# Moving the stage tiles and the weights' pool to multiples of 512 bytes in SBUF

## The chip, the cores and the metric

The kernel runs on one core of a Trainium2 chip. The metric is the device time of one execution in microseconds, the median of three runs. The engines of the core are TensorE (PE, with its weight loads listed apart as PEld), VectorE (DVE), ScalarE (ACT), GpSimd (POOL) and SyncE (SP), which here only issues DMAs. SBUF is the on-chip memory: 128 partitions, and in each of them a tile occupies a run of bytes that begins at some offset. All partitions of a tile use the same offset, so "address" in this document means the offset within a partition.

## The reference

Sparse attention with a local window and some global positions, followed by a feed-forward layer. For batch 8, 8 heads, 512 local and 32 global positions and head size 64:

```
s_g  = scale * q_g @ [k_g, k_l].T ;  out_g = softmax(s_g) @ [v_g, v_l]
s_l  = [scale * q_l @ k_g.T, scale * q_l @ k_l.T where |i - j| <= 32 else -1e9]
out_l = softmax(s_l) @ [v_g, v_l]
x = concat([out_g, out_l]) as 4608 tokens x 512
h = x @ w_in                      # 512 -> 2048
g = max(h, 0) + alpha * min(h, 0)
out = g @ w_out                   # 2048 -> 512
```

Everything is float32 in and out. The weights come to the kernel as 64-bit floats, and the kernel decodes them.

## The kernel before, in words

The feed-forward layer is the bulk of the work. Its tokens are handled in nine groups: one for each batch entry (512 columns) and one for all global positions (256 columns). Each group has 16 steps over the hidden size. In a step `f1` (line 395) computes 128 hidden features: twelve matmuls of 128 x 128 weights and 512 (or 256) moving columns into the PSUM tile `h_ps`. To keep float32 accuracy with a faster number format (`float32r`), each operand is split into a high and a low part: `xh` and `xl` for the activations, `wt[:, 0]` and `wt[:, 1]` for the weights; three products of the four are summed. DVE then applies the activation function (lines 407 and 408, tile `g`), ACT rounds it to `gh` (line 410), and POOL computes the remainder `gl` (line 411). Two steps later `f2` (line 414) multiplies `gh` and `gl` with the second weight matrix, twelve matmuls again, into four PSUM tiles `o0` to `o3` which accumulate over the 16 steps. At the end of a group they are copied to `ost` and written out.

The attention for the next groups runs between these steps. Its queries and keys arrive in `rawq` and `rawk` (line 156), are split into `hi` and `kl` (lines 186 to 199), and give scores of 192 or 224 columns (line 219). Probabilities lie in `p_sb` and, transposed, in `pt_sb`; the values lie in `vt`. For the first eight pairs of heads unsplit operands are used, from the tile `qk_raw` that shares the buffers of `hi`. The tile `gn` holds what the global queries need.

The weights are decoded while the first steps run: a DMA brings 64-bit words to `wraw` (line 105), ACT, DVE and POOL turn them into a float32 stage tile (lines 113 to 120), and `split_weights` (line 123) writes the high and the low part to `wt`. Both `wraw` and `wt` come from the weights' pool, 33 buffers of 4096 bytes per partition, which later also lends buffers to `rawk`.

The order of the instructions on each engine comes from a planner that simulates the program; parts of it are pinned to the written order (from step 36 on, line 561), and the attention's parts get a higher priority (line 551). All DMAs are issued from SP's queue.

Where a tile lies follows from the order of the pools and of the tiles in them, each size rounded up to 32 bytes. At the bottom are 256 bytes for DMA descriptors and four constants of 32 bytes each, so the first tile of the kernel, `alpha_sb`, lies at 384. Its 64 bytes are followed by `mask` (896), `p_sb` (7168), `pt_sb` (10240), `sg_sb` (1152), `x_raw` (8192) and `x_glb` (4096). Then come the 18 stage tiles of 2048 bytes (line 99: one tag `st` for `xh`, `xl`, `g`, `gh`, `gl`, `ost`, `vx`, and the weights under decoding), two buffers of 4864 for `hi`, nine small tiles of 32, `gn` (2432), `vt` (4096), six small tiles of 32 and three of 128, `rawq` (2048), two buffers of 2560 for `kl`, and last the pool of the weights. Added up, that gives:

| tile | address before | past a multiple of 512 |
|---|---|---|
| `p_sb`, `pt_sb`, `sg_sb` | 1344, 8512, 18752 | 320 |
| `x_raw`, `x_glb` | 19904, 28096 | 448 |
| stage tiles | 32192 + 2048 n | 448 |
| `hi`, two buffers | 69056, 73920 | 448, 192 |
| `gn` | 79072 | 224 |
| `vt` | 81504 | 96 |
| `rawq`, `kl` | 86176, 88224, 90784 | 160 |
| weights' pool | 93344 + 4096 n | 160 |

In `hi` the queries come first and the keys start 2048 bytes later; block i of the queries starts 512 i bytes in, and the four blocks of keys start 0, 128, 288 and 448 columns of 4 bytes in.

Of the kernel before, what the change touches and what calls it, by code (L numbers as in the profile page):

```python
# [8 lines left out]
F32 = mybir.dt.float32  # L9
# [10 lines left out]
NF = DF // 128  # L20
# [25 lines left out]
GS = (2, "mid")  # L46
EV = dict(pt0=(2, "mid"), pt1=(4, "pre"), ptg=(4, "pre"), pv0=(5, "mid"), pv1=(6, "mid"))
SM = (2, "post")
RATE = ((1, 1, 0), (2, 1))
GROUPS = [("l", b) for b in range(NB)] + [("g", 0)]  # L50

# [9 lines left out]
def longformer_ffn(ctx: ExitStack, tc: tile.TileContext, qk, qkr, gn, vt, vx, w, alpha, out):  # L61
# [3 lines left out]
    const = ctx.enter_context(tc.tile_pool(name="const", bufs=1))  # L65
    work = ctx.enter_context(tc.tile_pool(name="work", bufs=1))
# [1 line left out]

    dram = ctx.enter_context(tc.tile_pool(name="dram", bufs=1, space=bass.MemoryType.DRAM))
    wpool = ctx.enter_context(tc.tile_pool(name="wpool", bufs=NWB))  # L70
    alpha_sb = const.tile([128, NF], F32, name="alpha_sb")
    mask = const.tile([128, 224], F32, name="mask")
    p_sb = const.tile([128, 1792], F32, name="p_sb")
    pt_sb = const.tile([128, 2, 4, 2, 160], F32, name="pt_sb")
# [79 lines left out]
    raws, vts, vxs, gns = {}, {}, {}, {}  # L154
# [11 lines left out]
        raws[P, h, part] = raw  # L166

    def load_gn(P):
        gns[P] = work.tile([128, 608], F32, tag="gn", name="gn", bufs=1)
        b, p = divmod(P, NPAIR)  # L170
        nc.sync.dma_start(gns[P], gn[b, p])

# [97 lines left out]
    def global_softmax(P):  # L270
        s = gbank.pop(P)
        m, z = small("gm"), small("gz")
        nc.vector.tensor_reduce(m[:, 0:1], s[:, 0:288], axis=AX.X, op=ALU.max)
        nc.vector.tensor_scalar(m[:, 1:2], m[:, 0:1], -0.125, None, op0=ALU.mult)
        nc.vector.tensor_copy(m[0:64, 0:1], m[64:128, 1:2])
        nc.vector.tensor_tensor(m[0:64, 1:2], m[0:64, 1:2], m[0:64, 0:1], op=ALU.min)
        nc.vector.tensor_copy(m[64:128, 1:2], m[0:64, 1:2])
        nc.scalar.activation(sg_sb, s[:, 0:288], AF.Exp, bias=m[:, 1:2], scale=0.125, accum_out=z[:, 0:1])
        nc.vector.tensor_copy(z[0:64, 1:2], z[64:128, 0:1])
        nc.vector.scalar_tensor_tensor(z[0:64, 1:2], z[0:64, 1:2], 1e-9, z[0:64, 0:1], op0=ALU.add, op1=ALU.add)  # L280
        nc.vector.reciprocal(z[0:64, 1:2], z[0:64, 1:2])
        nc.vector.tensor_copy(z[64:128, 1:2], z[0:64, 1:2])
        nc.scalar.activation(sg_sb, sg_sb, AF.Copy, scale=z[:, 1:2])  # L283
# [90 lines left out]
    def pv_out(P, first, last):  # L374
        b, p = divmod(P, NPAIR)
        nc.scalar.copy(x_raw[:, p, 0:384].rearrange("d (i q) -> d i q", i=3), first[:, 0:480].rearrange("p (i q) -> p i q", i=3)[:, :, 0:128])
        nc.scalar.copy(x_raw[:, p, 384:512], last[:, 0:128])
        xg = x_glb[:, p, SG * b : SG * b + SG]
        nc.vector.tensor_reduce(xg, sub_ap(first, 0, 128, 128, ((1, 32), (160, 3))), axis=AX.X, op=ALU.add)
        nc.vector.tensor_tensor(xg, xg, last[:, 128:160], op=ALU.add)  # L380
# [60 lines left out]
    def live(P):  # L441
        return 0 <= P < NPR
# [3 lines left out]
    def glob(P, s, where):  # L446
        if GS == (s, where):
# [3 lines left out]
            elif P >= NRAW and (live(P) or live(P - 1)):  # L451
# [6 lines left out]
                if P > NRAW:  # L458
                    pv_out(P - 1, first, last)
        if live(P) and SM == (s, where):  # L460
            global_softmax(P)
# [34 lines left out]
    def attn_mid(u):  # L496
        P, s = divmod(u, 4)
        glob(P, s, "mid")
        while tails:
            tails.pop()()  # L500
        raw_events(u, "mid")
        if s == 0 and live(P):
            load_gn(P)
        if s == 0 and live(P + 1):
            if P + 1 < NRAW:
                load_pair(P + 1)
            else:
                load_qk(P + 1, 0, 0)
                load_qk(P + 1, 0, 1)
        if s == 1 and P == NRAW:  # L510
            for c0 in (0, 864):
                nc.gpsimd.memset(sub_ap(p_sb, 0, 128, c0, ((896, 2), (1, 32))), 0.0)
        if s == 2:
            if P == NRAW:
                nc.gpsimd.memset(sub_ap(pt_sb, 0, 128, 1280 + 512, ((640, 2), (1, 128))), 0.0)
            if live(P):
                load_v(P)
# [18 lines left out]
    def weights_step(u):  # L536
        k = state[0]
        n = RATE[0][u % len(RATE[0])] if u < NPRE else RATE[1][u % len(RATE[1])]
        new = [i for i in range(k, min(k + n, len(pieces)))]
# [120 lines left out]
```

## Time and profile before

| | us |
|---|---|
| median of three runs | 1040.6 (1039.6 to 1041.49) |
| span of the profiled execution, first to last instruction | 1038.9 |
| PE busy | 992.1 (96%) |
| DVE busy | 681.0 (66%) |
| ACT busy | 497.4 (48%) |
| POOL busy | 410.6 (40%) |
| mean granted PE clock | 0.977 |

The page's span is that of one profiled execution; the median lies 1.7 us above it. A busy time counts an instruction from its start to its end, and matmuls overlap, so how fast PE works is read from the distance between starts, not from the duration of one matmul. In a timeline row the first number is the start, the second the time from the first start to the last end of the merged instructions, and the count stands at the end. In a row of a group, the numbers after the bar are the busy time in us, the mean duration of one instruction in ns, and the idle time of the engine before them with what ended it.

### The profile page before, as it was taken

Reading aid. Unit: us, or ns where it says so; the run is one execution under the profiler, and the core shown is the slowest. Engines: PE = TensorE matmul, PEld = TensorE weight load, DVE = VectorE, ACT = ScalarE, POOL = GpSimd, SP = SyncE. Lnnn points to the kernel's source line nnn. Section 1 sums busy time; section 2 is a strip of 40 time slices with the busy share of each in tenths; the row PEclk is TensorE's granted clock in tenths of the full one; section 3 lists DMA queues with packets and bytes.
Section 4 is the critical chain, followed back from the end, with each engine's and each line's share of the span. In section 5 each row is a group of like instructions: output and inputs, shape, how many; then the busy total and the mean of one; then the engine's idle time right before and its main releaser. Section 6 shows DMA issues by size and latency. Waiting matters only on the chain.

```text
span 1038.9 us, 17103 instructions
## 1 busy us (share of the span) xinstructions
PE 992.1 (96%) x5592; PEld 791.2 (76%) x5592; DVE 681.0 (66%) x2162; ACT 497.4 (48%) x1331; POOL 410.6 (40%) x330
## 2 busy tenths in 40 slices
PE   6798989898999999999999999999999999999998
PEld 3455767676888878887888788878887788888798
DVE  8987788866666766676667666776667666322322
ACT  5466466665455554455455554555455543201121
POOL 6620466663344343333444433334443431122222
PEclk9896898998999999999999999999999999999999
DMA  9454232135444554455455555445445543100010
GB/s 335 175 187 172 103 126 86 56 94 161 148 148 141 160 149 148 140 161 157 148 149 151 165 150 148 141 149 151 148 144 159 146 126 92 41 1 1 1 42 21
DMA packets 95274, 133.00 MB, mean 128 GB/s; under 512 B 10192, under 2 KB 53712, under 8 KB 95184
## 3 DMA queue, kind: packets, MB, share of 16 engines
q1 hardware_dynamic: 95184, 131.91, 40.7%
q8 instruction: 44, 0.72, 0.3%
q14 instruction: 46, 0.38, 0.1%
HBM read 100.93 MB, written 30.93 MB: 127 GB/s over the span
## 4 chain that ended last, share of the span: by engine, by line
PE 77%; DVE 14%; DMA 3%; ACT 2%; issue 2%; POOL 1%; SPq 0%; ACTq 0%; DVEq 0%; POOLq 0%
PE o L93 33%; PE h_ps L93 31%; PE o_ps L93 6%; PE s_ps L93 4%; PE g_ps L93 3%; DVE wt L118 2%; DVE wt L115 2%; DVE rz L211 1%; DVE wt L117 1%; DMA rawq<-in_qk_dram 1%; DVE p_sb L246 1%; DVE g L408 1%; DMA out_dram<-ost 1%; DVE g L407 1%; DVE pt_sb L321 1%
## 5 line engine op out<-in xcount | busy, mean ns | idle before, releaser
L93 PE MATMUL h_ps<-xh,wt 128*128 128x512 f32 (+1 forms) x1152 | 352.2, 389 | 4.3 <-DVE g L408 3.9
L411 POOL TENSOR_TENSOR gl<-g,gh 128x512 fp32r<-128x512 f32 (+1 forms) x144 | 178.2, 1237 | 436.8 <-ACT gh L410 405.1
L93 PE MATMUL o<-gh,wt 128*128 128x512 f32 (+1 forms) x1152 | 282.4, 386 | 1.6 <-ACT ost L305 1.6
L93 PEld LDWEIGHTS o<-gh,wt 128*128 128x128 f32 x1152 | 204.5, 188 | 50.3 <-ACT ost L305 6.6
L93 PEld LDWEIGHTS h_ps<-xh,wt 128*128 128x128 f32 x1152 | 207.3, 191 | 44.6 <-DVE g L408 4.1
L93 PE MATMUL h_ps<-xl,wt 128*128 128x512 f32 (+1 forms) x576 | 222.6, 388 | 0.9 <-DVE xl L390 0.9
L410 ACT CAST gh<-g 128x512 fp32r<-128x512 f32 (+1 forms) x144 | 85.9, 596 | 266.4 <-DVE g L408 243.2
L407 DVE TENSOR_SCALAR g<-h_ps,alpha_sb 128x512 f32<-128x512 f32 (+1 forms) x144 | 103.2, 717 | 121.2 <-PE h_ps L93 120.4
L217 ACT ACTIVATE p_sb<-p_sb,rz 128x192 f32<-128x192 f32 (+1 forms) x252 | 101.3, 451 | 131.8 <-DVE rz L212 129.7
L93 PE MATMUL o<-gl,wt 128*128 128x512 f32 (+1 forms) x576 | 150.6, 382 | 0.0
L250 ACT ACTIVATE p_sb<-p_sb,mn 128x224 f32<-128x224 f32 (+2 forms) x256 | 115.0, 451 | 40.3 <-DVE mn L246 39.8
L93 PEld LDWEIGHTS h_ps<-xl,wt 128*128 128x128 f32 x576 | 109.3, 190 | 25.6 <-issue 1.3
L93 PEld LDWEIGHTS o<-gl,wt 128*128 128x128 f32 x576 | 104.5, 187 | 23.8 <-issue 0.5
L211 DVE TENSOR_SCALAR rz<-z 128x2 f32<-128x2 f32 x128 | 52.5, 411 | 91.3 <-ACT p_sb L250 90.2
L300 DVE STREAM_TRANSPOSE pt_sb<-sg_sb 32x64 f32<-32x64 f32 x384 | 90.7, 236 | 27.4 <-ACT sg_sb L283 21.2
L408 DVE SCALAR_TENSOR_TENSOR g<-h_ps,g 128x512 f32<-128x512 f32 (+1 forms) x144 | 93.9, 652 | 2.9
L196 POOL TENSOR_TENSOR hi<-rawq,hi 64x512 fp32r<-64x512 f32 x48 | 62.2, 1295 | 83.4 <-DMA vt<-in_vt_dram 50.0
L93 PE MATMUL o_ps<-pt_sb,vt 128*64 128x160 f32 (+4 forms) x832 | 72.3, 298 | 11.9 <-DVE mn L246 8.0
L199 POOL TENSOR_TENSOR kl<-rawk,hi 128x640 fp32r<-128x640 f32 x48 | 76.2, 1587 | 3.7
L93 PEld LDWEIGHTS o_ps<-pt_sb,vt 128*64 128x64 f32 (+2 forms) x832 | 50.3, 140 | 32.5 <-issue 12.2
L246 DVE CUSTOM_DVE_ANT_0 p_sb<-s_ps,mask 128x192 f32<-128x192 f32 x192 | 64.1, 362 | 11.1 <-PE s_ps L93 9.9
L120 POOL TENSOR_TENSOR wt<-wt,wr 128x512 int32<-128x512 int32 x32 | 43.2, 1352 | 66.2 <-DVE rz L211 38.1
(86 smaller groups left out, 1042.3 us busy)
## 6 DMA issues: line engine op xcount, KB each, us to landing
scratch<-p_sb SPq DMA_DIRECT2D x192, 112.0 KB, 2.3
wraw<-in_w_dram SPq DMA_DIRECT2D x32, 512.0 KB, 6.9
vt<-in_vt_dram SPq DMA_DIRECT2D x32, 512.0 KB, 5.0
rawk<-in_qk_dram SPq DMA_DIRECT2D x96, 160.0 KB, 2.9
rawq<-in_qk_dram SPq DMA_DIRECT2D x96, 128.0 KB, 2.7
pt_sb<-scratch SPq DMA_DIRECT2D x48, 256.0 KB, 2.8
gn<-in_gn_dram SPq DMA_DIRECT2D x32, 304.0 KB, 5.4
pt_sb<-scratch SPq DMA_DIRECT2D x48, 192.0 KB, 2.9
```

Source lines behind the costliest of these rows:

```text
L93: ins = nc.tensor.matmul(*a, **k)
L196: nc.gpsimd.tensor_tensor(q, raw[64:128], q.bitcast(F32), op=ALU.subtract)
L199: nc.gpsimd.tensor_tensor(kl[P, h], raw, t.bitcast(F32), op=ALU.subtract)
L211: nc.vector.tensor_scalar(rz[:parts, 0:n], z[:parts, 0:n], 1e-9, None, op0=ALU.add)
L217: nc.scalar.activation(r, r, AF.Copy, scale=rz[:parts, e : e + 1])
L246: nc.vector.tensor_tensor_reduce(out=pr, in0=s[:, 256 * e : 256 * e + nn], in1=masks[e], scale=-0.125, scalar=3.0e38, op0=ALU.add, op1=ALU ...
L250: nc.scalar.activation(pr, pr, AF.Exp, bias=mn[:, e : e + 1], scale=-1.0, accum_out=z[:, e : e + 1])
L300: nc.vector.transpose(dst, src)
L407: nc.vector.tensor_scalar(g[:, 0:n], h[:, 0:n], 0.0, alpha_sb[:, f : f + 1], op0=ALU.min, op1=ALU.mult)
L408: nc.vector.scalar_tensor_tensor(g[:, 0:n], h[:, 0:n], 0.0, g[:, 0:n], op0=ALU.max, op1=ALU.add)
L410: nc.scalar.copy(gh[:, 0:n], g[:, 0:n])
L411: nc.gpsimd.tensor_tensor(gl[:, 0:n], g[:, 0:n], gh[:, 0:n].bitcast(F32), op=ALU.subtract)
```

## The change

Two tiles are made larger, and only their first part is used, so that everything allocated behind them moves up: `alpha_sb` by 64 bytes and `gn` by 288. What is read and written, by which instruction, in which order and with which waits stays the same.

```
+PAD = (16, 72)
...
-    alpha_sb = const.tile([128, NF], F32, name="alpha_sb")
+    alpha_sb = const.tile([128, NF + PAD[0]], F32, name="alpha_sb")[:, 0:NF]
...
     def load_gn(P):
-        gns[P] = work.tile([128, 608], F32, tag="gn", name="gn", bufs=1)
+        gns[P] = work.tile([128, 608 + PAD[1]], F32, tag="gn", name="gn", bufs=1)[:, 0:608]
```

All tiles from `mask` to `gn` move by 64 bytes, those behind `gn` by 352. The stage tiles then begin at 32256, which is 63 x 512, and the weights' pool at 93696, which is 183 x 512; `rawq` and `kl` come to multiples of 512 too.

## The prediction

> **What bounds the kernel now.** I read the page's shares first, then the chain of waits, then the windows by stage.
>
> ```profile
> span 1038.9 us, 17103 instructions
> PE 992.1 (96%) x5592; PEld 791.2 (76%) x5592; DVE 681.0 (66%) x2162; ACT 497.4 (48%) x1331; POOL 410.6 (40%) x330
> PE 77%; DVE 14%; DMA 3%; ACT 2%; issue 2%; POOL 1%; SPq 0%; ACTq 0%; DVEq 0%; POOLq 0%
> ```
>
> ```profile
> 0.00:26.00 26.00, 16.33 (x77) 9.52 (x77) 21.06 (x50) 14.03 (x34) 17.94 (x31) 0.99 0.94 335
> 26.00:80.00 54.00, 46.41 (x338) 29.82 (x338) 48.95 (x175) 32.20 (x104) 23.81 (x17) 0.91 0.48 174
> ...
> 250.00:400.00 150.00, 148.14 (x834) 121.14 (x833) 100.68 (x346) 76.15 (x207) 57.16 (x42) 1.00 0.50 152
> 400.00:600.00 200.00, 196.23 (x1082) 160.11 (x1081) 139.09 (x478) 104.99 (x284) 79.26 (x58) 1.00 0.50 152
> ```
>
> The columns of the windows are length, busy time of PE, weight load, DVE, ACT and POOL, then granted clock, DMA share and GB/s. From 250 us on, PE is busy 98% of the time at a granted clock of 1.00, and nothing else passes 70%. Before that DVE leads in the first 80 us (21.06 of 26, 48.95 of 54), and DMA is close to full only in the first 26 (0.94). So an address can pay in two places: in how fast the matmuls run, and, for less, in the DVE and DMA work of the start.
>
> How fast do they run? The timeline of one step shows it.
>
> ```profile
> 262.62 0.65 PE L93 MATMUL h_ps<-xh,wt 128*128 128x512 f32 x2
> ...
> 265.44 2.03 PE L93 MATMUL o<-gh,wt 128*128 128x512 f32 x8
> 267.31 1.10 PE L93 MATMUL o<-gl,wt 128*128 128x512 f32 x4
> 268.24 0.25 PE L93 MATMUL s_ps<-hi 128*128 128x192 f32 x1
> ```
>
> Eight matmuls of 512 columns start between 265.44 and 267.31, four more by 268.24: twelve in 2.80 us, 233 ns each. The stage that warms the clock gives the rate at half clock:
>
> ```profile
> 29.04:32.02 2.98, 2.98 (x8) 1.88 (x7) 0.50 1.03 411
> ```
>
> Seven weight loads, so seven new matmuls of 512 columns, in 2.98 us is 426 ns each at a granted clock of 0.50; at full clock that would be 213 ns. The real spacing is 233, so **20 ns of each such matmul scale with something other than the clock**. The same holds at 256 columns, where DMA is silent:
>
> ```profile
> 1001.93 1.10 PE L93 MATMUL o<-gh,wt 128*128 128x256 f32 x8
> 1002.88 0.63 PE L93 MATMUL o<-gl,wt 128*128 128x256 f32 x4
> ```
>
> Eight in 0.95 us is 119 ns, against 106.5 (half of 213): 12 ns over. An excess that grows with the columns looks like the delivery of the moving operand, and this is what an address could touch.
>
> **The change part by part.** No instruction, wait or transfer is added, removed or moved in its queue; only offsets in a partition differ. Worked out from the tiles' sizes in order of allocation, the stage tiles (`xh`, `xl`, `g`, `gh`, `gl`, `ost`, `wt` and `wr` before the split) go from 448 past a multiple of 512 to 0; `wraw`, the split `wt`, `rawk`, `rawq` and `kl` from 160 to 0; the two `hi` buffers from 448 and 192 to 0 and 256; `p_sb`, `pt_sb`, `sg_sb` from 320 to 384; `vt` from 96 to 448; `gn` from 224 to 288. Each kind of access is priced by rows whose operands already lie at different offsets.
>
> *Weight loads.* They read `wt` at 160 (a multiple of 32 but not of 64) or a query in `hi` at 448 or 192 (multiples of 64):
>
> ```profile
> L93 PEld LDWEIGHTS h_ps<-xl,wt 128*128 128x128 f32 x576 | 109.3, 190 | 25.6 <-issue 1.3 <-DVE xl L390 1.1 <-DVE mn L246 0.2
> L93 PEld LDWEIGHTS o<-gl,wt 128*128 128x128 f32 x576 | 104.5, 187 | 23.8 <-issue 0.5
> L93 PEld LDWEIGHTS s_ps<-hi 128*128 128x128 f32 x192 | 36.4, 189 | 4.8 <-issue 0.5
> ```
>
> 187 to 190 ns at either offset, and beside a 233 ns matmul a load is hidden; its cover is the 233 - 190 = 43 ns left. Cost 0, and a gain is excluded by the cover.
>
> *ACT and POOL.*
>
> ```profile
> L410 ACT CAST gh<-g 128x512 fp32r<-128x512 f32 x128 | 79.4, 620 | 226.9 <-DVE g L408 206.4 <-DVE rz L212 12.9 <-DVE gz L281 2.9
> L193 ACT CAST hi<-rawq 128x512 fp32r<-128x512 f32 x48 | 29.6, 618 | 25.2 <-issue 13.7 <-PE s_ps L93 11.5
> L120 POOL TENSOR_TENSOR wt<-wt,wr 128x512 int32<-128x512 int32 x32 | 43.2, 1352 | 66.2 <-DVE rz L211 38.1 <-DVE wt L118 16.3 <-ACT p_sb L250 3.8
> L130 POOL TENSOR_TENSOR wt<-wt 128x512 fp32r<-128x512 f32 x32 | 43.0, 1347 | 23.0 <-DVE wt L127 10.7 <-issue 4.4 <-ACT wt L129 3.6
> ```
>
> 448 to 448 takes 620 ns (L410), 160 to 448 takes 618 (L193). On POOL, all operands at 448 take 1352 (L120), with operands at 448 and 160 it is 1347 (L130). Differences of 0.3 and 0.4%: no effect. Both engines also have slack in the PE stage. DVE has no clean pair of rows; with 0.4% on its 14% of the chain (145 us) the ends are -0.6 and +0.6 us, and I take 0.
>
> *DMA.*
>
> ```profile
> rawk<-in_qk_dram SPq DMA_DIRECT2D x96, 160.0 KB, 2.9
> ...
> pt_sb<-scratch SPq DMA_DIRECT2D x48, 256.0 KB, 2.8
> ```
>
> 160 KB to offset 160 land in 2.9 us, 256 KB to offset 320 in 2.8. On the chain DMA has 3%, 31 us; 0.1 in 2.9 of that is 1.1 us, so the ends are -1.1 and +1.1, and I take 0, since from 250 us on half of the DMA time is free and covers it. [...]
>
> *The moving operand.* This is the unknown. The first score matmul of a tile streams keys from `hi`, at offsets that can be told apart: the two heads alternate between the buffers at 448 and 192. Here are a first block at 192 (500.81), one at 448 (515.75), and a third block at 320 (509.73):
>
> ```profile
> 500.81 0.25 PE L93 MATMUL s_ps<-hi 128*128 128x192 f32 x1
> 500.90 0.28 PE L93 MATMUL s_ps<-kl,hi 128*128 128x192 f32 x1
> 501.01 0.28 PE L93 MATMUL s_ps<-hi 128*128 128x224 f32 x1
> 501.14 0.28 PE L93 MATMUL s_ps<-kl,hi 128*128 128x224 f32 x1
> ```
>
> ```profile
> 515.75 0.25 PE L93 MATMUL s_ps<-hi 128*128 128x192 f32 x1
> 515.84 0.28 PE L93 MATMUL s_ps<-kl,hi 128*128 128x192 f32 x1
> ```
>
> ```profile
> 509.73 0.27 PE L93 MATMUL s_ps<-hi 128*128 128x224 f32 x1
> 509.83 0.28 PE L93 MATMUL s_ps<-kl,hi 128*128 128x224 f32 x1
> ```
>
> 192 columns (768 B) from 192 cross one multiple of 512, from 448 two; both release the next matmul after 0.09 us. So moving by 256 bytes does nothing. But every offset seen here is 64 past a multiple of 128, and no quick matmul in this trace reads from a multiple of 128 or more. That leaves a gain open. Its end is the whole excess on the matmuls counted here (the other groups of 256 columns follow the same split, 128 + 64 + 128 + 64 = 384):
>
> ```profile
> L93 PE MATMUL h_ps<-xh,wt 128*128 128x512 f32 x1024 | 328.8, 402 | 4.3 <-DVE g L408 3.9 <-ACT xh L389 0.4
> L93 PE MATMUL o<-gh,wt 128*128 128x512 f32 x1024 | 264.7, 399 | 1.6 <-ACT ost L305 1.6
> L93 PE MATMUL h_ps<-xl,wt 128*128 128x512 f32 x512 | 204.5, 401 | 0.0
> L93 PE MATMUL o<-gl,wt 128*128 128x512 f32 x512 | 140.4, 395 | 0.0
> L93 PE MATMUL h_ps<-xh,wt 128*128 128x256 f32 x128 | 23.5, 280 | 0.0
> ```
>
> 3072 x 20 ns + 384 x 12 ns = 61.4 + 4.6 = 66 us at most. The other end is a loss of the same size, since nothing here excludes it. I take 0: the pair of rows that differs in offset (192 against 448) shows none.
>
> **The sum** is 1038.9 + 0 (weights) + 0 (ACT, POOL, DVE; ends 0.6) + 0 (DMA; ends 1.1) + 0 (moving operand; ends 66) = 1038.9. The median of the runs, 1040.6, lies 1.7 us above this span; so 1040.6, and 1.7 us either way for the small ends together.
>
> **The rivals.** (A) is the forecast: no change.
>
> (B) *The whole excess goes.* If the delivery of 512 columns is slowed because each piece of the stream begins off a boundary of 128 or more, at offset 0 the matmuls run at the clock: 1040.6 - 66 = 975. For it: the excess grows with columns and is absent at half clock. Against it: three offsets (192, 448, 320) with one rate per column. [...]
>
> (C) *One crossing less.* A row of 2048 B at 448 touches five blocks of 512 B and crosses four boundaries, at 0 it crosses three; with 256 columns two become one. If the excess is made of crossings, each costs 20 / 4 = 5 ns (12 / 2 = 6 at 256): 3072 x 5 + 384 x 6 = 17.7 us, so 1022.9. For it: the excess fits two and four crossings. Against it: the score matmuls above, with one and two crossings, both at 0.09.
>
> (D) *Slower: weights and moving operand come into step.* Now weights at 160 and stage tiles at 448 start 288 bytes apart; after, both at 0, and if the two reads meet in the same banks the stream stalls. For it: the 224 columns at 501.01, whose query and keys both start at 192, hold the next matmul for 0.13 us, those at 509.73, keys at 320 and query at 192, for 0.10. Against it: the 192 columns at 500.81 are in step too and take only 0.09, and the matmul at 501.01 follows a short one, so its weights may have been late. Of the 20 to 30 ns between these rows I give the step 5: 3072 x 5 + 384 x 5 = 17.3 us, so 1057.9. It decides from 0.7 ns per matmul on (0.2% of 1040.6 is 2.1 us, over 3072), since PE has no idle time to take it up.
>
> (E) *The tiles don't come to lie at multiples of 512,* because an allocation is rounded otherwise than I worked out: then nothing moves that matters, and the time is that of (A).
>
> **How the numbers follow.** What a measurement of this kernel can tell from no change is about 0.2%, 2.1 us; the own range of (A), 1038.5 to 1042.7, is that. (A) with (E) has 0.48: three engines and the weight loads show no effect of offset, and neither does the only pair for the moving operand. (C) has 0.18 and (B) 0.15, because an excess of 20 ns is there to be won and no multiple of 128 has been tried. (D) has 0.19: the same blank, the other sign. Faster is (B) + (C) = 0.33, the same 0.48, slower 0.19. The range leaves out (B) and the far part of (D): 1015 to 1056, which holds 0.48 + 0.18 and most of (D), about 0.81.
>
> **What would show it.** In the trace of the changed kernel: twelve matmuls of 512 columns in 2.80 us again (A), 2.57 (B), 2.74 (C) or 2.86 (D); eight of 256 columns in 0.95 (A). Weight loads at 187 to 191 ns; L193 and L410 within 1% of 618 and 620, L120 and L130 of 1352 and 1347; `wraw` landings and the DVE share of the first 80 us as now. The forecast is wrong if the step of twelve leaves 2.80 by more than 0.01 us, or if an engine beside PE shows another duration on tiles that moved and the start shifts with it.

## The result and the profile after

The changed kernel is **faster by 1.1%**: 1029.3 us median (1027.08 to 1031.62), against 1041.05 for the kernel before in the same comparison; the ratio is 0.9889 with a 95% interval of 0.987 to 0.9908. The forecast was no change.

The page of the changed kernel: span, the first row of busy times, and the chain of waits. (Line numbers are one higher than before, since the change adds a line.)

```profile
span 1029.8 us, 17103 instructions
PE 981.9 (95%) x5592; PEld 795.5 (77%) x5592; DVE 682.8 (66%) x2162; ACT 497.4 (48%) x1331; POOL 409.8 (40%) x330
PE 70%; DVE 14%; DMA 7%; issue 3%; ACT 2%; POOL 2%; SPq 1%; DVEq 0%; ACTq 0%; POOLq 0%
```

The span fell by 9.1 us and PE's busy time by 10.2; DVE, ACT and POOL kept theirs within 2 us, and the weight loads, which overlap the matmuls, have 4.3 us more. In the chain of waits DMA went from 3 to 7% and PE from 77 to 70%, but PE did not become idle for it: between 600 and 850 us it is busy 245.6 us, 246.2 before. The timeline of one step, as shown for before:

```profile
266.86 1.98 PE L94 MATMUL o<-gh,wt 128*128 128x512 f32 x8
268.67 1.07 PE L94 MATMUL o<-gl,wt 128*128 128x512 f32 x4
269.58 0.25 PE L94 MATMUL s_ps<-hi 128*128 128x192 f32 x1
```

Twelve matmuls of 512 columns start in 269.58 - 266.86 = 2.72 us, 227 ns each; before it was 2.80 us and 233 ns. At 256 columns it went the other way:

```profile
986.47 1.12 PE L94 MATMUL o<-gh,wt 128*128 128x256 f32 x8
987.43 0.64 PE L94 MATMUL o<-gl,wt 128*128 128x256 f32 x4
```

Eight in 0.96 us, 120 ns, against 0.95 and 119 before. Beside the matmuls only a DMA issue moved in a way that can be told from chance (the time to landing stands last):

```profile
scratch<-p_sb SPq DMA_DIRECT2D x192, 112.0 KB, 2.1
```

The weight load of `o<-gl` went from 187 to 189 ns, the ACT row of `hi<-rawq` from 618 to 619, the POOL row of the split from 1347 to 1344, and `rawk` stayed at 2.9 us. `scratch<-p_sb` was 2.3 us before: it reads `p_sb`, which moved from 320 to 384 past a multiple of 512. The five profiles with `p_sb` at 384 (the change, and e1, e6, e8 and e10 below) all have 2.1 us, the five with it at 320 or 352 all 2.3. It is no part of the gain, though: e1 has it and gains nothing, e3 and e7 lack it and gain all. Other landings differ by 0.1 to 0.4 us from profile to profile: `wraw` took 6.5 us in place of 6.9, but e1, whose weights still lie at 160, has 6.2, so its address is not shown to matter. So the gain is in how soon one matmul follows another.

**Why not more.** 3072 matmuls by 6 ns would be some 18 us; the spans differ by 9.1. The starts of the same matmuls in both traces tell where the rest went. Here are a step's `o<-gl` soon after 250 us and that of the last step of 512 columns, before and then after:

```profile
252.33 1.10 PE L93 MATMUL o<-gl,wt 128*128 128x512 f32 x4
...
991.11 1.10 PE L93 MATMUL o<-gl,wt 128*128 128x512 f32 x4
```

```profile
253.95 1.07 PE L94 MATMUL o<-gl,wt 128*128 128x512 f32 x4
...
981.25 1.07 PE L94 MATMUL o<-gl,wt 128*128 128x512 f32 x4
```

Between these two 738.78 us became 727.30, which is 11.5 us less; 1.6 us were lost ahead of them and 0.8 behind. The same stretch takes 727.28 and 727.32 us in e3 and e7 below, which gain as much, and 739.70 and 739.27 in e1 and e2, which gain nothing. The step at 369 us shows two of the reasons why the whole is less. Before, then after:

```profile
369.55 2.13 PE L93 MATMUL o<-gh,wt 128*128 128x512 f32 x8
371.52 1.10 PE L93 MATMUL o<-gl,wt 128*128 128x512 f32 x4
372.45 0.27 PE L93 MATMUL s_ps<-hi 128*128 128x224 f32 x1
```

```profile
369.61 2.11 PE L94 MATMUL o<-gh,wt 128*128 128x512 f32 x8
371.56 1.07 PE L94 MATMUL o<-gl,wt 128*128 128x512 f32 x4
372.47 0.27 PE L94 MATMUL s_ps<-hi 128*128 128x224 f32 x1
```

First, at 369 us the changed kernel is not ahead at all; all of the net gain comes in the 670 us behind. What the start gives differs from profile to profile: at the `o<-gl` of 252.33 us the change is 1.6 us behind, e3 1.3 behind, e7 0.6 ahead, and e1, without any gain per matmul, 1.7 ahead. In the start PE waits for DVE and for loads (in the changed kernel up to 250 us, 4.5 us for `mn` and 4.1 for `g`, and 5.0 for the load of `qk_raw`) and its granted clock falls below 1.00 (0.84 from 80 to 156 us, in both); that a faster matmul there only waits longer is likely, but not shown. Second, these twelve follow the attention's plain float32 matmuls, and gain only 0.04 us (2.90 to 2.86) where those in an undisturbed step gain 0.08: after such a stretch, in the changed kernel at 369.61 us, one gap of 336 ns (335 before) and six of 228 to 236 come ahead of the first of 227. Two smaller things take some back: PE now reaches the end of a group earlier than ACT has emptied the accumulators, and its wait for `ost` ahead of `o<-gh` grew from 1.6 to 3.1 us, and the 256-column stage lost 384 x 2 ns, under 1 us.

```profile
L94 PE MATMUL o<-gh,wt 128*128 128x512 f32 x1024 | 259.3, 394 | 3.1 <-ACT ost L306 3.1
```

### The profile page after: what moved, and what is told of

It reads as the page before. It is cut to its first block, busy times and chain, and to the rows that moved or that the text cites. A ratio compares the mean times of both kernels' runs of the same rounds, so it can differ in the third digit from the quotient of the medians.

```text
span 1029.8 us, 17103 instructions
## 1 busy us (share of the span) xinstructions
PE 981.9 (95%) x5592; PEld 795.5 (77%) x5592; DVE 682.8 (66%) x2162; ACT 497.4 (48%) x1331; POOL 409.8 (40%) x330
## 4 chain that ended last, share of the span: by engine, by line
PE 70%; DVE 14%; DMA 7%; issue 3%; ACT 2%; POOL 2%; SPq 1%; DVEq 0%; ACTq 0%; POOLq 0%
PE h_ps L94 28%; PE o L94 28%; PE o_ps L94 6%; PE s_ps L94 4%; PE g_ps L94 3%; DMA rawq<-in_qk_dram 2%; DVE pt_sb L301 2%; DVE wt L119 2%; DVE wt L116 1%; DMA rawk<-in_qk_dram 1%; DMA gn<-in_gn_dram 1%; DVE wt L118 1%; DVE g L408 1%; DVE p_sb L247 1%; DVE g L409 1%
## 5 line engine op out<-in xcount | busy, mean ns | idle before, releaser
L94 PE MATMUL h_ps<-xh,wt 128*128 128x512 f32 (+1 forms) x1152 | 348.4, 386 | 4.4 <-DVE g L409 4.1
L94 PE MATMUL o<-gh,wt 128*128 128x512 f32 (+1 forms) x1152 | 277.3, 382 | 3.1 <-ACT ost L306 3.1
L94 PE MATMUL h_ps<-xl,wt 128*128 128x512 f32 (+1 forms) x576 | 220.2, 384 | 0.9 <-DVE xl L391 0.9
L411 ACT CAST gh<-g 128x512 fp32r<-128x512 f32 (+1 forms) x144 | 85.9, 596 | 256.8 <-DVE g L409 231.9
L212 DVE TENSOR_SCALAR rz<-z 128x2 f32<-128x2 f32 x128 | 54.9, 429 | 92.7 <-ACT p_sb L251 91.5
```

Source lines behind the costliest of these rows:

```text
L94: ins = nc.tensor.matmul(*a, **k)
L212: nc.vector.tensor_scalar(rz[:parts, 0:n], z[:parts, 0:n], 1e-9, None, op0=ALU.add)
L411: nc.scalar.copy(gh[:, 0:n], g[:, 0:n])
```

## The experiments

Three theories stood at first: (W) the weights' address decides, since 160 is not a multiple of 64; (M) the moving operand's address decides; (S) the distance between the two decides. "Distance" is the moving operand's address less the weights'; the expectations of e1 and e2 count it the other way round, weights less moving operand. The first four kernels only change the two pads.

**One operand at a time, and both at 448.**

```
e1_stage       PAD = (16, 112)   # stage tiles 0, weights 160: distance 352
e2_weights     PAD = (0, 88)     # stage tiles 448, weights 0: distance 448
e3_w448        PAD = (0, 72)     # both 448: distance 0
e4_s480_w160   PAD = (8, 120)    # stage tiles 480, weights 160: distance 320
```

> Only the stage tiles move to a multiple of 512; the weights' pool stays 160 past one. Theory W (the weights' address decides: a load that starts 32 past a multiple of 64 slows the matmul that streams beside it): as before, twelve matmuls of 512 columns in 2.80 us, about 1041 us. Theory M (the moving operand's address decides): as after, 2.72 us, about 1029 us. Theory S (the distance between the two addresses decides, which must be a multiple of 64): distance 160, as before, 2.80 us, about 1041 us.

> Only the weights' pool (with rawq and kl) moves to a multiple of 512; the stage tiles stay 448 past one. Theory W: 2.72 us for twelve matmuls, about 1029 us. Theory M: 2.80 us, about 1041 us. Theory S: distance 64, so 2.72 us, about 1029 us.

> The stage tiles stay at 448 past a multiple of 512, and the weights' pool moves to 448 too: nothing lies at a multiple of 512, but all at multiples of 64. If multiples of 64 are enough (theories W and S): 2.72 us for twelve matmuls, about 1029 us. If it takes multiples of 512, or the moving operand's address decides (theory M): 2.80 us, about 1041 us.

> The stage tiles move to 480 and the weights' pool stays at 160: both 32 past a multiple of 64, and 320 apart. Theory S: the distance is a multiple of 64, so 2.72 us for twelve matmuls, about 1029 us. Theory W: as before, 2.80 us, about 1041 us. Theory M: not faster than before, 2.80 us or more, 1041 us or more.

| kernel | stage tiles, weights | distance modulo 256 | twelve of 512 columns | median, us | ratio to before (95%) |
|---|---|---|---|---|---|
| before | 448, 160 | 32 | 2.80 | 1039.47 | |
| e1_stage | 0, 160 | 96 | 2.80 | 1042.31 | 1.0026 (1.001 to 1.0041) |
| e2_weights | 448, 0 | 192 | 2.80 | 1039.44 | 1.0004 (0.9988 to 1.0019) |
| e3_w448 | 448, 448 | 0 | 2.72 | 1031.34 | 0.9911 (0.9886 to 0.9936) |
| e4_s480_w160 | 480, 160 | 64 | 2.75 | 1033.94 | 0.9942 (0.9921 to 0.9963) |

Moving either operand alone to a multiple of 512 gains nothing (e1 is even a little slower); putting both at 448 gains what the change gains. W and M fall: each had one of e1 and e2 fast. Of S remains that the distance decides, but not as I had put it: a distance of 448 is a multiple of 64 and gave nothing, and 320 gave a part. The timelines of e2 and of e4:

```profile
402.33 2.03 PE L94 MATMUL o<-gh,wt 128*128 128x512 f32 x8
404.20 1.09 PE L94 MATMUL o<-gl,wt 128*128 128x512 f32 x4
405.13 0.25 PE L94 MATMUL s_ps<-hi 128*128 128x192 f32 x1
```

```profile
399.76 1.99 PE L94 MATMUL o<-gh,wt 128*128 128x512 f32 x8
401.59 1.08 PE L94 MATMUL o<-gl,wt 128*128 128x512 f32 x4
402.51 0.25 PE L94 MATMUL s_ps<-hi 128*128 128x192 f32 x1
```

**The cost by itself.** A kernel with nothing but matmuls and their weight loads, so that no other engine reads SBUF.

```
+    def section(name, m, wo, n, times):   # moving at m, weights at wo past a multiple of 512
...
+        for k in range(times):
+            q = wo // 4 + 128 * (k % 8)
+            nc.tensor.matmul(ps[:, 0:n], wv[:, q : q + 128], mv[:, m // 4 : m // 4 + n], ...)
...
+    for k in range(16): section("wide_" + letters[k], 0, (512 - 32 * k) % 512, 512, 48)
...
+    for k in range(16): section("thin_" + letters[k], 0, (512 - 32 * k) % 512, 256, 64)
```

> All of the kernel's work is left out; only matmuls and their weight loads run, in sections of 48 (512 columns) or 64 (256 columns), each with a weight load of 128 columns. Sections wide_a to wide_p and thin_a to thin_p have the moving operand at a multiple of 512 and the weights 0, 32, ... 480 bytes short of one, so that the distance (moving less weights) is 0, 32, ... 480. Five sections named abs repeat the pairs of addresses of the four kernels before and of the first one. Theory D (the distance of the two reads of TensorE, modulo 512, sets the pace, whatever the other engines do): 227 ns per matmul at distance 0 and for 448 with 448, 233 for 448 with 160, 448 with 0 and 0 with 160, and 230 for 480 with 160; at 256 columns 120 ns at distance 0 and 113 at 320 and 448. Theory O (the reads collide with those of other engines): all sections alike, whatever the distance.

Its timeline; the next section's start less a section's own, over the count, is the time per matmul:

```profile
11.80 11.05 PE L79 MATMUL wide_a<-mv,wv 128*128 128x512 f32 x48
22.69 11.35 PE L79 MATMUL wide_b<-mv,wv 128*128 128x512 f32 x48
33.88 11.16 PE L79 MATMUL wide_c<-mv,wv 128*128 128x512 f32 x48
44.88 11.36 PE L79 MATMUL wide_d<-mv,wv 128*128 128x512 f32 x48
...
100.92 11.05 PE L79 MATMUL wide_i<-mv,wv 128*128 128x512 f32 x48
111.81 11.35 PE L79 MATMUL wide_j<-mv,wv 128*128 128x512 f32 x48
...
190.04 11.06 PE L79 MATMUL abs_same<-mv,wv 128*128 128x512 f32 x48
200.94 11.36 PE L79 MATMUL abs_prior<-mv,wv 128*128 128x512 f32 x48
212.14 11.15 PE L79 MATMUL abs_half<-mv,wv 128*128 128x512 f32 x48
223.13 11.35 PE L79 MATMUL abs_wonly<-mv,wv 128*128 128x512 f32 x48
```

Distance 0 (wide_a) gives 10.89 / 48 = 226.9 ns, 32 gives 233.1, 64 gives 229.2, and 256 (wide_i) gives 226.9 again; 288 (wide_j) takes the 11.35 us of wide_b. The sections at the addresses of the real kernels give 227.1 (448 with 448), 233.3 (448 with 160, the kernel before) and 229.0 (480 with 160). All of it appears with the other engines idle, so theory O, collisions with their reads, falls: **at 512 columns the addresses of the two operands of TensorE itself set the pace, by their distance modulo 256 bytes**. The period is 256 and not 512. All weights of a section lie at the same offset, so this does not tell whether a matmul's own weights count or those that are loaded beside it for the next one.

**32 bytes instead of 352.**

```
-PAD = (16, 72)
+PAD = (0, 8)      # stage tiles stay at 448, weights at 192: distance 256
```

> The kernel before with 32 bytes more behind gn and nothing else: stage tiles at 448 as before, the weights' pool at 192, so nothing that matters lies at a multiple of 512, and the distance is 256. The distance theory with a period of 256: twelve matmuls of 512 columns in 2.72 us and about 1030 us, like the change. If the period is 512, or addresses at multiples of 512 are what counts: 2.80 us and about 1041 us.

1029.78 us, ratio 0.9897 (0.9875 to 0.9918): the same gain, with neither operand at a multiple of 512, and the weights' pool (with `vt`, `rawq` and `kl`) moved by 32 bytes. Its timeline:

```profile
400.03 1.98 PE L94 MATMUL o<-gh,wt 128*128 128x512 f32 x8
401.84 1.07 PE L94 MATMUL o<-gl,wt 128*128 128x512 f32 x4
402.75 0.25 PE L94 MATMUL s_ps<-hi 128*128 128x192 f32 x1
```

Beside it the changed kernel was run once more on the same chip:

> The changed kernel once more, to stand beside the other two on one chip: ratio to the kernel before 0.987 to 0.991, about 1029.5 us.

1028.64 us, ratio 0.9889 (0.9866 to 0.9911), as in the first comparison.

**The rest of the excess.** Even 227 ns is 13.5 above the clock's 213 (an estimate: half of the 427 ns from start to start at a granted clock of 0.50). Does the weight load take that?

```
+    for name, d in (("four", 4), ("eight", 8), ("sixteen", 16), ...): section("by_" + name, 0, (512 - d) % 512, 512, 48)
+    for name, d in (("zero", 0), ("half", 128)):
+        for cols, c in (("full", 128), ("two", 64), ("one", 32)):
+            section(f"load_{name}_{cols}", 0, (512 - d) % 512, 512, 48, c)    # c columns of weights
```

> Matmuls and weight loads alone again, all other work left out. Distances of 4, 8, 16, 48, 80 and 112 bytes at 512 columns; then, at distances 0 and 128, weight loads of 128, 64 and 32 columns; then 384 moving columns at distances 0, 128 and 192. If the weight load takes the time from the stream (theory D): the excess over 213 ns falls with the columns loaded, from 13.5 (distance 0) and 20 (128) at 128 columns to about a half at 64 and a quarter at 32. If the stream itself is slow (theory R, a rate of its own at full clock): the excess stays whatever is loaded. The small distances: if the reads meet in pieces of 32 bytes or more, 4, 8 and 16 bytes give the 226.7 of distance 0; if each byte counts, something between that and 233.

```profile
12.08 11.05 PE L79 MATMUL by_four<-mv,wv 128*128 128x512 f32 x48
22.97 11.36 PE L79 MATMUL by_eight<-mv,wv 128*128 128x512 f32 x48
34.16 11.13 PE L79 MATMUL by_sixteen<-mv,wv 128*128 128x512 f32 x48
45.13 11.30 PE L79 MATMUL by_fortyeight<-mv,wv 128*128 128x512 f32 x48
...
78.52 11.05 PE L79 MATMUL load_zero_full<-mv,wv 128*128 128x512 f32 x48
89.41 11.20 PE L79 MATMUL load_zero_two<-mv,wv 128*64 128x512 f32 x48
100.45 11.29 PE L79 MATMUL load_zero_one<-mv,wv 128*32 128x512 f32 x48
111.57 11.30 PE L79 MATMUL load_half_full<-mv,wv 128*128 128x512 f32 x48
122.71 11.18 PE L79 MATMUL load_half_two<-mv,wv 128*64 128x512 f32 x48
133.73 11.23 PE L79 MATMUL load_half_one<-mv,wv 128*32 128x512 f32 x48
```

With 64 columns of weights the matmuls at distance 0 take 230.0 ns, with 32 they take 231.7: no less than with 128 (226.9). At distance 128 they take 232.1 with 128 columns, 229.6 with 64 and 230.6 with 32, a little less, where theory D of this run expected the excess over 213 to fall to a half and a quarter. So the load's length does not pay for the excess, and theory D of this run falls; what the remaining excess is made of stays open. A distance of 4 bytes still gives 226.9, 8 gives 233.1, 16 gives 228.5 and 48 gives 231.9, so this is no matter of pieces of 32 bytes or more either.

**The last stage, 256 columns.** The sections named thin had shown 113.3 ns at a distance of 192 and 119.8 at 0, so I shifted the global group's tiles within their buffers, first by 192 bytes, then by 448, the address at which e2 ran fast.

```
+SHIFT = 48          # e10_shift448: 112
...
+        o = 0 if kind == "l" else SHIFT
+        xh, xl = stage("xh", F32R)[:, o : o + n], stage("xl", F32R)[:, o : o + n]
...
+        gh, gl = stage("gh", F32R)[:, s : s + n], stage("gl", F32R)[:, s : s + n]
```

> The changed kernel, and besides, for the global group alone, xh, xl, gh and gl use columns 48 to 303 of their stage tiles in place of 0 to 255, so that the moving operand starts 192 bytes past the weights modulo 256. The distance theory with the period of 256 that the sections showed: 384 matmuls of 256 columns at 113.4 ns in place of 120, 2.5 us less than the changed kernel, about 1027 us against about 1029.5; eight of them in 0.91 us. If the distance does nothing at 256 columns in the whole kernel: 0.96 us for eight and the changed kernel's time.

> As e6_shift, but the global group uses columns 112 to 367, so that the moving operand starts 448 bytes past a multiple of 512 with the weights at 0: the pair of addresses at which e2_weights ran 113.4 ns per matmul of 256 columns. If the pair of addresses decides (modulo 512, not only their distance modulo 256): 113.4 ns, eight in 0.91 us, 384 x 6.5 ns = 2.5 us less than the changed kernel, about 1026.5 us. If it is something else in e2_weights: 118 to 120 ns and about 1029 us.

Both missed. The stage of e2, then of e10:

```profile
993.42 1.07 PE L94 MATMUL o<-gh,wt 128*128 128x256 f32 x8
994.33 0.62 PE L94 MATMUL o<-gl,wt 128*128 128x256 f32 x4
```

```profile
987.00 1.10 PE L95 MATMUL o<-gh,wt 128*128 128x256 f32 x8
987.94 0.63 PE L95 MATMUL o<-gl,wt 128*128 128x256 f32 x4
```

e10, and e6 too, take 0.94 us for eight, 117.5 ns: better than the change's 120, not the 113 expected, which e2 has (0.91 us). The times, 1028.39 us for e6 (ratio 0.9887, 0.9869 to 0.9906) and 1030.42 for e10 (0.9907, 0.9891 to 0.9923), can't be told from the changed kernel's. The last kernel moves the other operand of the two:

> Matmuls and weight loads alone, all other work left out. The weights stay at a multiple of 512, and the moving operand starts 0, 32, ... 480 bytes past one, at 512 columns (wide_a to wide_p) and at 256 (thin_a to thin_p). If the distance modulo 256 alone decides: at 512 columns 227 ns at 0 and 256, 229 at 64 and 320, 233 to 234 else, as when the weights were moved; at 256 columns 113 at 192 and 448 and 117 to 120 else. If the moving operand's own address counts too: the 256 columns at 192 differ from those at 448. The last section, short_words, has both operands in 16-bit words: if the stream is held up by bytes per column, its matmuls of 512 columns take 213 to 216 ns and no excess.

```profile
12.74 9.23 PE L79 MATMUL wide_a<-mv,wv 128*128 128x512 f32 x40
21.81 9.50 PE L79 MATMUL wide_b<-mv,wv 128*128 128x512 f32 x40
31.15 9.33 PE L79 MATMUL wide_c<-mv,wv 128*128 128x512 f32 x40
40.31 9.49 PE L79 MATMUL wide_d<-mv,wv 128*128 128x512 f32 x40
...
195.50 5.82 PE L79 MATMUL thin_g<-mv,wv 128*128 128x256 f32 x48
201.16 5.84 PE L79 MATMUL thin_h<-mv,wv 128*128 128x256 f32 x48
...
252.38 8.81 PE L97 MATMUL short_words<-mb,wb 128*128 128x512 bf16 x40
```

At 512 columns the rule holds whichever operand is moved: 226.8 ns at distance 0, 233.5 at 32, 229.0 at 64. At 256 columns it doesn't: a distance of 192 made by moving the stream gives 5.66 / 48 = 117.9 ns, made by moving the weights it gave 113.3, and in the whole kernel 448 less 0 gave 113 once (e2, where the stage tiles themselves lay at 448) and 117.5 once (e10). e4, at a distance of 64, ran 113 too, where the section at 64 gave 117.8. The 256-column matmuls fall into one of several rhythms, and which one is not given by the two addresses modulo 512 alone. What gives it stays open.

In 16-bit words the same stream takes about (8.81 - 0.39) / 39 = 216 ns: the clock's 213 with 3 more. It is an estimate, since 0.39 us for the last matmul is worked out from wide_a, 9.23 - 39 x 0.2268. So the excess is nearly gone with 16-bit words; whether the width or the number format does it was not separated, and only distance 0 was run. For `float32r` this case shows 227 at best.

## Why the prediction was wrong

- **The bound** was read rightly: PE sets the pace from 250 us on, 20 ns of each matmul are not the clock's, and this excess is what an address touched (6 to 7 of the 20). The small terms (weight load, ACT, POOL, DMA, DVE) came out at 0 for the time, as put down; one DMA did land sooner at its new address (`scratch<-p_sb`, 2.3 to 2.1 us), in runs with and without a gain.
- **The step that failed is the price of the moving operand**, "I take 0: the pair of rows that differs in offset (192 against 448) shows none". That pair could not show it, for two reasons that the runs brought out. Its queries and keys lie in the same tile, so the distance between the two reads is the same in both buffers; and the two offsets differ by 256, which is just the period. It measured no change of the quantity that decides. The term was 0 us; with the distance at 0, the stretch from 252 to 991 us measured -11.5.
- Behind it lies a wrong form of the question: each operand was priced by its own address. The weight load was put at 0 because its duration doesn't depend on the address (it doesn't: 187 to 192 ns) and because it is hidden. Its address counted all the same, in the pace of the matmuls: with the stage tiles at 448, a step's twelve took 2.80 us with the weights at 160 or 0, and 2.72 with them at 448 or 192.
- **Rival (C)** gave 5 ns per matmul and 1022.9 us. The size was near (6 to 7 ns in an undisturbed step), but its mechanism, crossings of 512, is refuted: e1 has one crossing less and no gain, e3 and e7 have four crossings and all of it. Its sum was too large for the reasons shown above: no gain up to 369 us, half of it after the attention's matmuls, and a loss at 256 columns where it had put a gain.
- **Rival (D)** named the right pair, the weights' read and the stream coming into step, with the wrong sign: in step (distance 0) is the fast case. The rows I took for it, 0.13 us at 501.01, followed short matmuls, as the text said.
- **Rival (B)**, the whole excess, did not come: none of the distances tried at 512 columns went below 226.6. **Rival (E)** falls too, since the step left 2.80 us as the worked-out addresses have it in all kernels; no view shows an address itself.

## What to carry to other kernels

When PE runs 512-column `float32r` matmuls back to back, compare the distance between starts with the clock's 213 ns for 512 columns (the estimate from 427 ns at a granted clock of 0.50), and look at the addresses of moving operand and weights as a pair: the same offset modulo 256 bytes ran 227 ns here, most other distances 233. At 256 columns and fewer the runs show no such rule. One 32-byte pad was enough for the 1%; no tile had to be aligned. And a pair of rows proves "no effect" only if the quantity in question differs between them.

## What the runs showed of the hardware that was not expected

- Start to start of 512-column matmuls in `float32r`, by the distance modulo 256: 226.7 to 227.3 ns at 0, 229 at 64, 232 to 234.4 at the other multiples of 32; at 4 bytes 227, at 8 233, at 16 228.5.
- At half the clock the excess is gone, at a distance of 32 as well: before, the nine `h_ps` matmuls from 246.24 to 250.08 us start 427 ns apart at a granted clock of 0.50, twice 213. (The row at 29.04 us that the prediction used holds `warm` matmuls, whose operands both begin at the start of one tile, so at distance 0.)
- The short score matmuls on `kl` moved from a distance of 224 or 96 to 0 or 128 with the change, and one of 192 columns releases the next after 0.12 us as before (268.32 to 268.44 before, 269.66 to 269.78 after).
- After the attention's plain float32 matmuls one gap of 336 ns and six of 228 to 236 come first (the changed kernel, 369.61 us), then 227; the twelve there took 2.86 us, those of an undisturbed step 2.72. What the matmuls settle into was not shown.
- Loading fewer weights hardly changes the pace, and not one way: 230.0 and 231.7 ns with 64 and 32 columns against 226.9 with 128 at distance 0; 229.6 and 230.6 against 232.1 at distance 128.
- A DMA that reads 112 KB from `p_sb` landed in 2.1 us with the tile at 384 past a multiple of 512, and in 2.3 with it at 320 or 352, in ten profiles without exception.
